# The first x tile of a gated S5/MLP kernel: two feature slabs by plain loads and TensorE transposes, three by one DMA transpose, and W1's first block loaded in two halves

## The chip, the cores and the metric

The kernel runs on one core of a Trainium2 chip. The metric is the device time in microseconds (us) of one execution; lower is better. The kernel before takes a median of 214.95 us in three runs (214.95 to 215.01). In a profile, times are counted from the start of the core's span, and the span is about 1.3 us shorter than the metric.

## The reference

```python
x = A_x                                               # (1, 2048, 640), bf16
g = sigmoid((x * gate_w).sum(-1, keepdims=True))
a = S5(x)        # complex diagonal state-space scan: x @ B, h = Lam*h + u, h @ C, + x * Dskip
b = gelu(x @ w1 + b1) @ w2 + b2                       # w1 (640, 1728), w2 (1728, 640)
return g * a + (1 - g) * b
```

Only the first product matters here: `x @ w1` for the first 512 rows of x. The contraction runs over the 640 features, which must lie on the partitions. So x has to be transposed: five slabs of 128 features by 512 rows.

## The kernel before

All work is put into a list with priorities and estimated durations. A small scheduler orders each engine's instructions at build time, and semaphore waits are put where needed. The parts that the change touches are these (cuts marked `# ...`).

```python
# xT[q]: x tile q transposed, [128, 5 slabs, 512]; xn: x untransposed; FW = 8 * 128 columns of W1
def xtrans(q, ks, prio, dur):        # DMA transpose of the slabs ks, on SP's queue
    load_T(..., [(xT[q][:, ks[0]:ks[-1]+1, :], x2[q*512:(q+1)*512, ks[0]*128:(ks[-1]+1)*128])], ...)

def w1load(k, eng, prio):            # block k of W1: 128 features, 1024 columns, 256 KB
    load(f"w1_{k}", eng, ..., W1sb[:, k, 0:FW], B_w1[k*128:(k+1)*128, 0:FW], [("w1", k)], ...)

w1load(0, "act", -101)
xtrans(0, [0], 0, 1.27)
xtrans(0, [1, 2], 1, 1.27)
w1load(1, "sp", 2)
w1load(2, "sp", 3)
xtrans(0, [3, 4], 4, 1.27)
w1load(3, "sp", 5)
w1load(4, "sp", 6)
# the last 704 columns of W1, all five blocks, 880 KB, in one load:
load("w1_r", "sp", "l_w1r", W1sb[:, :, FW:F], B_w1[:, FW:F].rearrange("(k p) f -> p k f", p=128), [("w1", "r")], ...)
# ... then, on the same queue, the DMA transposes of BT and further loads

def f_warm():                        # eight matmuls on a zeroed tile wz
    for _ in range(8):
        t = nc.tensor.matmul(PS[6][:, :], wz[:, 0:128], wz[:, :], start=True, stop=True)
# ...
def m1_first():                      # stage 1: 40 matmuls, block k outermost, 8 PSUM banks open
    seq = [(k, jf) for k in range(KD) for jf in range(NW)]
    seq.remove((0, NW - 1)); seq.insert(seq.index((1, NW - 1)), (0, NW - 1))
    for k, jf in seq:
        ...  # PS[jf] += W1sb[:, k, jf].T @ xT[0][:, k, :]     needs slab k and block k
def m1(q, j0=0):                     # stage 2 begins with m1(0, 8): the last 704 columns, needs w1_r
    ...
```

I call the matmuls of stage 1 with slab k "k=0" to "k=4", and `w1_r` "W1's last part". PSUM is the memory in which TensorE sums its products, in eight banks. Stage 1 opens all eight at once, so that it can use each slab and block of W1 as it comes. Because k=0 uses seven banks first (bank 7 holds the transposed parameter rows for a while), nine matmuls come between the start of k=1 and that of k=2.

## Time and profile before

| | before |
|---|---|
| median of the runs | 214.95 us |
| TensorE's matmul rows busy | 210.0 of 213.8 us |
| first W1 matmul (k=0) | 4.82 us |
| k=1 starts | 7.39 us |
| k=2 starts | 9.33 us |
| stage 2 starts | 14.51 us |
| W1's last part lands | 13.01 us |

The page of the profile, its line of busy times (PE is TensorE's matmuls, PEld its weight loads, DVE is VectorE, ACT is ScalarE, POOL is GpSimd; further on, SPq is the sync engine issuing DMAs, and "issue" is time for which the profile shows no wait):

```profile
span 213.8 us, 3098 instructions
PE 210.0 (98%) x1257; PEld 119.3 (56%) x1257; DVE 188.3 (88%) x260; ACT 112.9 (53%) x205; POOL 2.5 (1%) x10
```

The chain of waits of the kernel before, restricted to the first 20 us (start in us, length in us, what):

```profile
0.68 0.07 issue
0.75 1.23 SPq L332
1.97 0.06 issue
2.03 1.29 SPq L332
3.32 0.05 issue
3.37 3.89 DMA W1sb<-in_B_w_dram
7.26 0.14 issue
7.39 7.28 PE ps L598 x33
14.67 5.40 PE ps L618 x25
```

L332 is the DMA transpose on SP's queue, L598 is stage 1, and L618 is stage 2. Read it from the top: two transposes are issued, then W1's second block is issued and lands 3.89 us later, and from 7.39 us there is only TensorE, down to 211.61 us.

The waits of TensorE, and its instructions in order of time at the head, say the same (columns of the first: who waits for whom, us in total, times, longest; of the second: start, length, what, and in brackets the idle time before it):

```profile
PE ps L400 <- DVE wz L393: 1.2, 1, 1.2
PE ps L598 <- DMA W1sb<-in_B_w_dram: 0.4, 1, 0.4
```

```profile
4.82 2.13 PE L598 MATMUL ps<-xT,W1sb 128*128 128x512 bf16 x7
6.79 0.22 PE L410 MATMUL ps<-ident,rows 128*128 128x128 bf16 x1
7.39 7.28 PE L598 MATMUL ps<-xT,W1sb 128*128 128x512 bf16 x33 [0.39 <-DMA W1sb<-in_B_w_dram]
14.51 0.81 PE L618 MATMUL ps<-xT,W1sb 128*128 128x512 bf16 x3
```

From 7.39 us on TensorE does not pause: 33 matmuls at 216 ns from start to start end stage 1 at 14.51 us.

Two things are not on a page and are read from the single records of the trace throughout: when each load's last completion event came (its "landing"), and the matmuls' start-to-start times. The latter tell the clock: 427 ns for 512 columns is half rate, 216 ns is full rate. In this profile the last half-rate W1 matmul starts at 5.21 us.

### The profile page before, as it was taken

What the parts mean: (1) busy time and instruction counts of PE and PEld (TensorE: products, weight loads), DVE (VectorE), ACT (ScalarE), POOL (GpSimd) and SP (SyncE); (2) the same over time, 40 slices, a digit from 0 to 9 for tenths busy, and PEclk for the clock granted to TensorE, in tenths of its full rate; (3) what the DMA queues carried; (4) which work ended last, traced back from release to release, by engine and by line L of the source; (5) the groups of instructions that cost most, each with busy time, mean ns of one, the idle gap of its engine ahead of it and who ended that gap; (6) DMA issues with size and microseconds to landing.
All of it is one profiled execution on the core that took longest, in us unless ns stands there. A gap on an engine that the chain in (4) does not pass through costs nothing.

```text
span 213.8 us, 3098 instructions
## 1 busy us (share of the span) xinstructions
PE 210.0 (98%) x1257; PEld 119.3 (56%) x1257; DVE 188.3 (88%) x260; ACT 112.9 (53%) x205; POOL 2.5 (1%) x10
## 2 busy tenths in 40 slices
PE   7999999999999999999999999999999999999995
PEld 2344444444567675444467767444446777677673
DVE  1599999999999899999999999499999999988612
ACT  2569556679525334557835332556786554535230
POOL 1000000000000100000000010000000000000000
PEclk9999999999999999999999999999999999999999
DMA  7999699999000140000000023000000010000011
GB/s 138 297 271 192 142 364 271 224 191 204 0 0 3 61 153 3 31 0 0 0 3 31 0 49 138 32 0 0 3 0 2 0 34 31 31 34 31 31 34 31
DMA packets 30874, 16.35 MB, mean 76 GB/s; under 512 B 23948, under 2 KB 29964, under 8 KB 30860
## 3 DMA queue, kind: packets, MB, share of 16 engines
q1 hardware_dynamic: 30368, 14.57, 28.7%
q0 software_dynamic: 288, 1.31, 2.0%
q10 hardware_dynamic: 204, 0.27, 0.5%
q8 instruction: 10, 0.16, 0.4%
q14 instruction: 4, 0.03, 0.0%
HBM read 7.63 MB, written 2.62 MB: 48 GB/s over the span
## 4 chain that ended last, share of the span: by engine, by line
PE 95%; DMA 2%; SPq 1%; DVE 0%; issue 0%
PE ps L745 26%; PE ps L618 22%; PE ps L791 21%; PE ps L658 20%; PE ps L598 3%; DMA W1sb<-in_B_w_dram 2%; PE ps L759 1%; SPq L332 1%; PE ps L636 1%; DVE osb L824 0%
## 5 line engine op out<-in xcount | busy, mean ns | idle before, releaser
L745 PE MATMUL ps<-W2sb,Gl 128*128 128x320 bf16 x416 | 59.1, 299 | 0.0
L745 PEld LDWEIGHTS ps<-W2sb,Gl 128*128 128x128 bf16 x416 | 40.6, 98 | 16.5 <-ACT Gl L625 0.4
L618 PE MATMUL ps<-xT,W1sb 128*128 128x512 bf16 x220 | 48.1, 379 | 0.0
L791 PE MATMUL ps<-CT,H 128*128 128x320 bf16 x320 | 46.1, 299 | 0.0
L698 DVE TENSOR_TENSOR_SCAN W<-atab,V 128x1280 bf16<-128x1280 f32 x16 | 44.3, 2811 | 0.3
L658 PE MATMUL ps<-xT,BT 128*128 128x512 bf16 x200 | 43.8, 379 | 0.0
L773 ACT ACTIVATE E<-ps,g1col 128x320 bf16<-128x320 f32 x32 | 16.1, 526 | 42.2 <-PE ps L759 18.3
L791 PEld LDWEIGHTS ps<-CT,H 128*128 128x128 bf16 x320 | 30.7, 98 | 13.5 <-issue 1.8
L618 PEld LDWEIGHTS ps<-xT,W1sb 128*128 128x128 bf16 x220 | 21.5, 98 | 25.9
L625 ACT ACTIVATE Gl<-ps,cols 128x512 bf16<-128x512 f32 x44 | 29.7, 691 | 11.5 <-PE ps L618 11.5
L658 PEld LDWEIGHTS ps<-xT,BT 128*128 128x128 bf16 x200 | 19.4, 98 | 23.5 <-ACT Gl L625 0.4
L667 ACT ACTIVATE U<-ps 128x512 bf16<-128x512 f32 x40 | 23.6, 595 | 15.7 <-PE ps L658 15.6
L802 ACT ACTIVATE E<-ps,gcol 128x320 bf16<-128x320 f32 x30 | 15.7, 528 | 16.7 <-PE ps L791 16.6
L732 ACT ACTIVATE ps<-b2b 128x320 f32<-128x320 bf16 x32 | 14.0, 440 | 0.9
L460 DVE TENSOR_TENSOR osb<-xg,E 128x640 bf16<-128x640 bf16 x15 | 7.3, 487 | 7.8 <-ACT E L802 6.8
L810 DVE SCALAR_TENSOR_TENSOR xg<-xn,gcol,dsk 128x640 bf16<-128x640 bf16 x16 | 13.8, 882 | 0.4
L575 DVE SCALAR_TENSOR_TENSOR scr<-xn,gwb 128x640 bf16<-128x640 bf16 x16 | 13.2, 823 | 0.4
L460 DVE TENSOR_TENSOR H<-H,V 128x1280 bf16<-128x1280 bf16 x16 | 12.5, 821 | 0.3
L460 DVE TENSOR_TENSOR V<-V,W 128x1280 bf16<-128x1280 bf16 x16 | 12.5, 821 | 0.3
L460 DVE TENSOR_TENSOR V<-mr,U 128x2560 bf16<-128x2560 bf16 x8 | 11.9, 1489 | 0.2
L460 DVE TENSOR_TENSOR H<-c,W 128x2560 bf16<-128x2560 bf16 x8 | 11.9, 1488 | 0.1
L460 DVE TENSOR_TENSOR V<-s,W 128x2560 bf16<-128x2560 bf16 x8 | 11.9, 1484 | 0.0
(77 smaller groups left out, 101.2 us busy)
## 6 DMA issues: line engine op xcount, KB each, us to landing
out_dram<-osb SPq DMA_DIRECT2D x15, 160.0 KB, 1.8
W2sb<-in_B_w_dram SPq DMA_DIRECT2D x1, 2080.0 KB, 12.2
xn<-in_A_x_dram SPq DMA_DIRECT2D x2, 640.0 KB, 6.4
xn<-in_A_x_dram POOLq DMA_DIRECT2D x2, 640.0 KB, 4.8
W1sb<-in_B_w_dram SPq DMA_DIRECT2D x4, 256.0 KB, 4.1
W1sb<-in_B_w_dram SPq DMA_DIRECT2D x1, 880.0 KB, 6.1
W1sb<-in_B_w_dram ACTq DMA_DIRECT2D x1, 256.0 KB, 2.8
gwb<-in_gate_w_dram SPq DMA_DIRECT2D x1, 160.0 KB, 5.2
```

What stands on the lines that cost most here:

```text
L460: return inc("dve", nc.vector.tensor_tensor(out=o, in0=a, in1=b, op=o_))
L618: t = nc.tensor.matmul(PS[bank][:, :], W1sb[:, k, jf * 128:(jf + 1) * 128], xT[q][:, k, :], start=(k == 0), stop=(k == KD - 1))
L625: return inc("act", nc.scalar.activation(Gl[q % 2][:, jf, :], PS[bank][:, :], ACT.Gelu_apprx_tanh, bias=b1col[:, jf:jf + 1]))
L658: t = nc.tensor.matmul(PS[bank][:, :], BT[:, ci, kd, k * 128:(k + 1) * 128], xT[q][:, kd, :], start=(kd == 0), stop=(kd == KD - 1))
L667: return inc("act", nc.scalar.activation(dst, src, ACT.Copy, scale=1.0 if ci == 0 else -1.0))
L698: t = inc("dve", nc.vector.tensor_tensor_scan(out=g[:, ci, :], data0=a, data1=v[:, ci, :], initial=0.0, op0=ALU.mult, op1=ALU.add))
L732: return inc("act", nc.scalar.activation(PS[bank][:, 0:HALF], b2b[:, cols], ACT.Copy))
L745: t = nc.tensor.matmul(PS[bank][:, 0:HALF], Gl[q % 2][:, jf, t4 * 128:(t4 + 1) * 128], W2sb[:, jf, cols], start=False, stop=False, skip_gr ...
L773: return inc("act", nc.scalar.activation(E1[c % NE][:, cols], PS[bank][:, 0:HALF], ACT.Copy, scale=g1col[:, c:c + 1]))
L791: t = nc.tensor.matmul(PS[bank][:, 0:HALF], H[b % NHB][:, ci, k, s * 128:(s + 1) * 128], CT[:, ci, k, cols], start=(i == 0), stop=(i == 2 ...
L802: return inc("act", nc.scalar.activation(E2[c % NE][:, cols], PS[bank][:, 0:HALF], ACT.Copy, scale=gcol[:, c:c + 1]))
L810: return inc("dve", nc.vector.scalar_tensor_tensor(out=xg[c % 2][:, :], in0=xn[q % 2][:, c % 4, :], scalar=gcol[:, c:c + 1], in1=dsk[:, :] ...
```

## The change

The intent is to start the useful TensorE work earlier. A DMA transpose takes long from issue to landing (4.03 us for slab 0), and the transposes stand in front of W1 in SP's queue. So slabs 0 and 1 are loaded plainly and transposed by TensorE, which is idle then. The other three slabs come by one DMA transpose after W1's blocks 1 and 2. The warm-up matmuls take a constant in place of a zeroed tile and so need not wait.

```diff
-        w1load(0, "act", -101)
-        xtrans(0, [0], 0, 1.27)
-        xtrans(0, [1, 2], 1, 1.27)
-        w1load(1, "sp", 2)
-        w1load(2, "sp", 3)
-        xtrans(0, [3, 4], 4, 1.27)
-        w1load(3, "sp", 5)
-        w1load(4, "sp", 6)
+        KN = 2
+        def xnat(k, prio):           # one slab, untransposed: 512 runs of 256 B
+            load(f"xna{k}", "sp", ..., xn[0][:, :, k*128:(k+1)*128], x2[0:512, k*128:(k+1)*128]...)
+        xnat(0, 0)
+        for h in range(2):           # W1's first block in two halves of 512 columns
+            load(f"w1_0{h}", "sp", ...)
+        xnat(1, 1.2)
+        w1load(1, "sp", 1.3)
+        w1load(2, "sp", 2)
+        xtrans(0, range(KN, KD), 3, 1.8)
+        w1load(3, "sp", 4)
+        w1load(4, "sp", 5)
 ...
-            for _ in range(8): matmul(PS[6], wz, wz)
+            for n in (512, 512, 512, 512, 512, 256): matmul(PS[5][:, 0:n], one, one)
+        for k in range(KN):          # 4 transposes of 128 columns into a PSUM bank, then a copy
+            ... nc.tensor.transpose(pt[:, c*128:(c+1)*128], xn[0][:, c, k*128:(k+1)*128], ident)
+            ... nc.vector.tensor_copy(out=xT[0][:, k, :], in_=pt)
+        ... one filler matmul on the constant, between slab 0's transposes and k=0
 ...
-        xnload(0, "sp", prio=32.4)
+        load("xnb", ...)             # the other three slabs of the untransposed x
```

Behind these loads the queue is unchanged: W1's last part, then the transposes of BT.

More of the change, by code (lines that the diff above doesn't have):

```diff
@@ L350, in w1load @@
             load(f"w1_{k}", eng, f"l_w1{k}", W1sb[:, k, 0:FW], B_w1[k * 128:(k + 1) * 128, 0:FW], [("w1", k)], prio=prio, lat=2.6)
-        w1load(0, "act", -101)
-        xtrans(0, [0], 0, 1.27)
-        xtrans(0, [1, 2], 1, 1.27)
-        w1load(1, "sp", 2)
-        w1load(2, "sp", 3)
-        xtrans(0, [3, 4], 4, 1.27)
-        w1load(3, "sp", 5)
-        w1load(4, "sp", 6)
+        KN = 2
+        def xnat(k, prio):
+            load(f"xna{k}", "sp", f"l_xna{k}", xn[0][:, :, k * 128:(k + 1) * 128],
+                 x2[0:512, k * 128:(k + 1) * 128].rearrange("(c p) d -> p c d", p=128), [("xna", k)], prio, dur=0.45, lat=2.0)
+        xnat(0, 0)
+        for h in range(2):
+            fs = slice(h * FW // 2, (h + 1) * FW // 2)
+            load(f"w1_0{h}", "sp", f"l_w10{h}", W1sb[:, 0, fs], B_w1[0:128, fs], [("w1", 0, h)], 0.1 + h, dur=0.45, lat=2.0)
+        xnat(1, 1.2)
[4 more added lines that the diff above has]
+        w1load(4, "sp", 5)
         load("w1_r", "sp", "l_w1r", W1sb[:, :, FW:F], B_w1[:, FW:F].rearrange("(k p) f -> p k f", p=128), [("w1", "r")], prio=20, lat=5.0)
@@ L388, in bass_gated_mix__ssm_conv_s5__dense_activation_gelu__prompt_kernel, with f_xt, f_xc, f_fill @@
         op("const", "dve", 0.8, ["iota"], ["ident"], f_const, prio=-65)
-        wz = SB("wz", [128, 512], BF16)
-        def f_wz():
-            return inc("dve", nc.vector.memset(wz[:, :], 0.0))
-        op("wz", "dve", 0.35, (), ["wz"], f_wz, prio=-70)
+        one = nc.const_aps.tensor(1.0, [128, 1], BF16)
         def f_warm():
             t = None
-            for _ in range(8):
-                t = nc.tensor.matmul(PS[6][:, :], wz[:, 0:128], wz[:, :], start=True, stop=True)
+            for n in (512, 512, 512, 512, 512, 256):
+                t = nc.tensor.matmul(PS[5][:, 0:n], one.broadcast_to([128, 128]), one.broadcast_to([128, n]), start=True, stop=True)
             return inc("pe", t)
-        op("warm", "pe", 3.2, ["wz"], [("bank", 6)], f_warm, prio=-1000)
+        op("warm", "pe", 2.5, (), [("bank", 5)], f_warm, prio=-1000)
+        for k in range(KN):
+            bank = 7 - k
+            pt = PS[bank][:, :].bitcast(BF16)[:, 0:512]
+            def f_xt(k=k, pt=pt):
+                t = None
+                for c in range(4):
+                    t = nc.tensor.transpose(pt[:, c * 128:(c + 1) * 128], xn[0][:, c, k * 128:(k + 1) * 128], ident[:, :])
+                return inc("pe", t)
+            op(f"xt{k}", "pe", 0.44, [("xna", k), "ident"], [("bank", bank)], f_xt, prio=(-990, 4.5)[k])
+            def f_xc(k=k, pt=pt):
+                return inc("dve", nc.vector.tensor_copy(out=xT[0][:, k, :], in_=pt))
+            op(f"xc{k}", "dve", 0.42, [("bank", bank)], [("xT", 0, k)], f_xc, prio=-2000 + k)
+        def f_fill():
+            return inc("pe", nc.tensor.matmul(PS[5][:, :], one.broadcast_to([128, 128]), one.broadcast_to([128, 512]), start=True, stop=True))
+        op("fill", "pe", 0.4, (), [("bank", 5)], f_fill, prio=-980)
         XT = {q: [("xT", q, k) for k in range(KD)] for q in range(NQ)}
@@ L410, in f_cols @@
             return inc("pe", nc.tensor.transpose(psC, rows[:, :], ident[:, :]))
-        op("cols", "pe", 0.3, list(ROWS) + ["b1b", "ident"], [("bank", 7)], f_cols, prio=7.5)
+        op("cols", "pe", 0.3, list(ROWS) + ["b1b", "ident"], [("bank", 7)], f_cols, prio=9.5)
         def f_cols1():
@@ L547, in bass_gated_mix__ssm_conv_s5__dense_activation_gelu__prompt_kernel @@
         load("gwb", "sp", "l_gwb", gwb[:, :], gate_w.partition_broadcast(128), ["gwb"], prio=32.2)
-        xnload(0, "sp", prio=32.4)
+        load("xnb", "sp", "l_xnb", xn[0][:, :, KN * 128:D], x2[0:512, KN * 128:D].rearrange("(c p) d -> p c d", p=128),
+             [("xn", 0, 0), ("xn", 0, 1)], 32.4, dur=1.0, lat=6.0, reads=[("xna", 0), ("xna", 1)])
         load("w2a", "sp", "l_w2a", W2sb[:, 0:NF - 1, :], B_w2[0:nmain, :].rearrange("(j p) d -> p j d", p=128), ["w2a"], prio=33, lat=8.0)
@@ L599, in f_mm @@
                                                       start=(k == 0), stop=(k == KD - 1)))
-                op(f"m1_0_{jf}_{k}", "pe", d_mm(512), [("xT", 0, k), ("w1", k)], [("bank", jf)] ,
+                op(f"m1_0_{jf}_{k}", "pe", d_mm(512), [("xT", 0, k), ("w1", k) if k else ("w1", 0, jf // (NW // 2))], [("bank", jf)] ,
                    f_mm, prio=pe_prio())
@@ L620, in f_mm @@
                     return inc("pe", t)
-                op(f"m1_{q}_{jf}", "pe", KD * d_mm(512), XT[q] + ([("w1", k) for k in range(KD)] if jf < NW else [("w1", "r")]), [("bank", bank)], f_mm, prio=pe_prio())
+                op(f"m1_{q}_{jf}", "pe", KD * d_mm(512), XT[q] + ([("w1", 0, 0), ("w1", 0, 1)] + [("w1", k) for k in range(1, KD)] if jf < NW else [("w1", "r")]), [("bank", bank)], f_mm, prio=pe_prio())
                 def f_ge(jf=jf, bank=bank):
```

## The prediction

> **What bounds the kernel now.** In the chain of waits TensorE runs from 7.39 us to 211.61 us as an unbroken row of matmul groups (PE is 95% of the chain; the engine table says PE 210.0 of 213.8 us). The view of who waited for whom has only two waits of PE, both in the head. So only the head can move the time: before 7.39 us the chain is two DMA-transpose issues (0.75 to 3.3 us) and the load of W1's second block (issued 3.37, landed 7.26). Later engines have room: each H tile is ready at least 3.2 us before its first matmul, each bias-primed bank at least 3.4 us (times in the trace). What the head saves should arrive whole.
>
> **The head before.** Warm-up matmuls 1.20 to 4.8 us, 427 ns start to start (full clock from 5.76 us). x slab 0 (issued 0.75) lands at 4.78; seven k=0 matmuls 4.81 to 6.8; a wait; k=1 from 7.39. At 216 ns per matmul, nine matmuls later, k=2 starts at 9.33; x slabs 3 and 4 (landed 9.03) are just in time. 24 matmuls of the first stage follow without a gap. The question: when does k=2 start after the change?
>
> **What the change does.** It adds 8 transposes of 128 columns, two PSUM copies on VectorE (estimate 0.4 to 0.6 us each) and one filler matmul, all ahead of the stream that binds. It removes the zeroing of the warm-up tile (warm-up starts about 0.45 us sooner) and two DMA-transpose issues of 1.23 us each at the front of the SP queue. W1's first block moves from ACT's queue to SP in halves.
>
> Estimates from the trace's durations: plain issues cost 0.4 to 0.57 us; the first plain load landed 2.84 us after issue. So:
> - slab 0 (issued 0.75) lands at 3.2 to 3.6; transposed and copied near 4.4.
> - W1's halves land near 3.8 and 4.3, slab 1 near 4.8, W1 block 1 near 5.6 (before 7.26), block 2 near 6.3.
> - k=0 runs 4.4 to 6.6 (partly at half clock), k=1 until about 8.5: TensorE could start k=2 then.
> - The three-slab transpose is issued near 4.05. Before, two slabs landed 4.47 us after issue; a third adds about 0.6 us (512 packets of 256 B, 18 ns each, 16 engines), less some queueing behind W1: landing 8.5 to 9.2. **This, not W1 or slab 0, decides k=2**: about 8.9, against 9.33.
>
> W1 blocks 3 and 4 follow 0.7 us apart and stay ahead of k=3 and k=4, 1.73 us apart.
>
> The Trainium skill ("DMA: Bandwidth & Descriptors", Specifications) asks 512 B or more for line rate; the plain slabs use 256 B runs, so they may be slower than I assume; no run here shows it yet.
>
> **Predicted time.** Saving about 0.45 us: **214.5 us**, range **213.95 to 215.05**. Faster by over 2% 0.01, within 2% 0.98, slower 0.01.
>
> **What would show it.** First W1 matmul near 4.4 us (was 4.81); k=1 near 6.6 (was 7.39) with no wait for W1; a wait for the three-slab transpose before k=2, which starts near 8.9; then one unbroken chain of unchanged length (202.3 us). W1's second block gone from the chain, the transpose in its place.
>
> **What would make it wrong.** Slow 256 B loads, so slab 0 comes no earlier; the three-slab transpose landing after 9.3 (a loss) or before 8.4 (then TensorE's own work decides, saving up to 0.9 us); full clock not granted before 5.8 us, so that k=0 and k=1 run at half rate; VectorE's reordered stages running out of their 3 us of room.

## The result, and the profile after

| | runs | median us | range | ratio to before | 95% interval |
|---|---|---|---|---|---|
| before | 4 | 214.98 | 214.95 to 215.29 | | |
| changed | 4 | 215.07 | 214.76 to 215.18 | 0.9999 | 0.9981 to 1.0016 |

A ratio here is the mean time of one kernel's fast runs (all but those over 1.5% above its fastest) over the mean of the other's fast runs in the same rounds, so it is not quite the ratio of the two medians. The saving of 0.45 us did not show, and the median fell 0.02 us above the top of the predicted range (the ratio, put on the 214.95 us of before, gives 214.93, inside it). The forecast ratio, 214.5 to 214.95 or 0.9979, lies just below the interval.

The profile after is of the execution of 215.18 us. The page's line of busy times has hardly moved:

```profile
span 213.9 us, 3103 instructions
PE 209.4 (98%) x1254; PEld 119.4 (56%) x1264; DVE 188.6 (88%) x261; ACT 113.4 (53%) x205; POOL 2.5 (1%) x10
```

TensorE in order of time at the head; L624 is stage 1 now, L644 stage 2, L415 the slab transposes, L435 the parameter rows:

```profile
4.32 1.04 PE L624 MATMUL ps<-xT,W1sb 128*128 128x512 bf16 x4 [0.15 <-DVE xT L421]
5.19 0.39 PE L415 MATMUL ps<-ident,xn 128*128 128x128 bf16 x4
5.41 1.07 PE L624 MATMUL ps<-xT,W1sb 128*128 128x512 bf16 x3
6.72 0.60 PE L624 MATMUL ps<-xT,W1sb 128*128 128x512 bf16 x2 [0.24 <-DMA W1sb<-in_B_w_dram]
7.17 0.22 PE L435 MATMUL ps<-ident,rows 128*128 128x128 bf16 x1
7.22 7.03 PE L624 MATMUL ps<-xT,W1sb 128*128 128x512 bf16 x30
14.54 0.82 PE L644 MATMUL ps<-xT,W1sb 128*128 128x512 bf16 x3 [0.28 <-DMA W1sb<-in_B_w_dram]
```

The waits of TensorE (two lines left out, 0.8 us before the warm-up and 0.2 us of "issue" later), and the end of the chain's head (same columns as before):

```profile
PE ps L644 <- DMA W1sb<-in_B_w_dram: 0.3, 1, 0.3
PE ps L624 <- DMA W1sb<-in_B_w_dram: 0.2, 1, 0.2
PE ps L624 <- DVE xT L421: 0.2, 1, 0.2
```

```profile
7.30 0.04 issue
7.35 7.14 DMA W1sb<-in_B_w_dram
14.49 0.05 issue
14.54 5.57 PE ps L644 x25
```

The times of the first part came out as forecast. The first W1 matmul starts at 4.32 us (forecast 4.4), k=1 at 6.72 us (6.6), the three-slab transpose lands at 8.85 us, and k=2 starts at 8.89 us (8.9; before 9.33). That is 0.44 us gained. The group of 30 at 7.22 us hides a short pause before k=2; the view merges it.

One of these agreements is luck. The prediction had W1's second block landing near 5.6 us and no wait for W1 at k=1. The block landed at 6.68 us, and TensorE waited for it, as the bracket at 6.72 us shows. That k=1 still came near the forecast is because k=0 was through sooner: no matmul of it ran at half rate, and its seventh started at 6.10 us, so k=1 could have followed at 6.32.

Then comes what the forecast did not have. Stage 1's last matmul starts at 13.87 us, and stage 2 could follow at 14.09 (one step of 216 ns). It starts at 14.53, because the load issued at 7.35 us, W1's last part, took 7.14 us and landed at 14.49. Before, the same load landed at 13.01. The bracket says 0.28 us and not 0.44, because the profile's modelled end of a matmul lies after the next one could start. The gain of 0.44 us at k=2 is given back at stage 2: 14.53 against 14.51 us. From there to the end, both take the same time: 215.15 − 14.51 = 200.64 us before, 215.18 − 14.53 = 200.65 us after.

So the arithmetic fits in one execution of each. The open questions were whether the late landing belongs to the change or to chance, whether removing that wait returns the gain, and whether anything else stands in the way. I had three candidates:

- **Order.** The new order of loads makes W1's last part land late each time.
- **Scatter.** That landing scatters in every kernel; the kernel before has about 1.5 us of room for it in the one profile and the changed one has less.
- **Elsewhere.** The gain is also lost to something other than that landing.

### The profile page after: what moved, and what is told of

It reads as the page before. It is cut to its first block, busy times and chain, and to the rows that moved or that the text cites. A ratio compares the mean times of both kernels' runs of the same rounds, so it can differ in the third digit from the quotient of the medians.

```text
span 213.9 us, 3103 instructions
## 1 busy us (share of the span) xinstructions
PE 209.4 (98%) x1254; PEld 119.4 (56%) x1264; DVE 188.6 (88%) x261; ACT 113.4 (53%) x205; POOL 2.5 (1%) x10
## 4 chain that ended last, share of the span: by engine, by line
PE 92%; DMA 3%; SPq 3%; issue 1%; DVE 0%
PE ps L771 26%; PE ps L644 22%; PE ps L817 21%; PE ps L684 20%; DMA W1sb<-in_B_w_dram 3%; SPq L325 2%; PE ps L785 1%; PE ps L662 1%; SPq L332 1%; DVE osb L850 0%
## 5 line engine op out<-in xcount | busy, mean ns | idle before, releaser
L644 PE MATMUL ps<-xT,W1sb 128*128 128x512 bf16 x215 | 47.6, 379 | 0.5 <-DMA W1sb<-in_B_w_dram 0.3
L684 PE MATMUL ps<-xT,BT 128*128 128x512 bf16 x196 | 43.1, 379 | 0.3 <-issue 0.2
L644 PEld LDWEIGHTS ps<-xT,W1sb 128*128 128x128 bf16 x220 | 21.5, 98 | 26.5 <-DMA W1sb<-in_B_w_dram 0.8
L651 ACT ACTIVATE Gl<-ps,cols 128x512 bf16<-128x512 f32 x44 | 29.8, 690 | 11.9 <-PE ps L644 11.9
L485 DVE TENSOR_TENSOR V<-mr,U 128x2560 bf16<-128x2560 bf16 x8 | 11.9, 1490 | 0.2
L485 DVE TENSOR_TENSOR H<-c,W 128x2560 bf16<-128x2560 bf16 x8 | 11.9, 1488 | 0.1
L485 DVE TENSOR_TENSOR V<-s,W 128x2560 bf16<-128x2560 bf16 x8 | 11.9, 1484 | 0.0
```

The costliest lines, as they stand in the source:

```text
L485: return inc("dve", nc.vector.tensor_tensor(out=o, in0=a, in1=b, op=o_))
L644: t = nc.tensor.matmul(PS[bank][:, :], W1sb[:, k, jf * 128:(jf + 1) * 128], xT[q][:, k, :], start=(k == 0), stop=(k == KD - 1))
L651: return inc("act", nc.scalar.activation(Gl[q % 2][:, jf, :], PS[bank][:, :], ACT.Gelu_apprx_tanh, bias=b1col[:, jf:jf + 1]))
L684: t = nc.tensor.matmul(PS[bank][:, :], BT[:, ci, kd, k * 128:(k + 1) * 128], xT[q][:, kd, :], start=(kd == 0), stop=(kd == KD - 1))
```

## The experiments

All kernels gave correct results. The three calls ran on two chips: runs 1 to 8 on one, 9 to 12 on another.

### 1 and 2. b_again and a_again: both kernels unchanged, second profiles

> The kernel before, unchanged, for a second profile. Both theories: 214.95 to 215.0 us. Theory A (the last part of W1 lands late only because of the changed order of loads): it lands near 13.0 us again, 1.5 us ahead of the matmuls that need it at 14.5. Theory B (the landing of that part scatters from execution to execution whatever the order): it lands somewhere from 12.9 to 14.5, and the total does not move, because there is 1.5 us of room.

> The changed kernel, unchanged, for a second profile. k=2 starts at 8.9 us again, the first W1 stage ends at 14.08, and the total is about 200.5 us plus the later of 14.08 and the landing of W1's last part. Theory A: that landing is again at 14.3 to 14.5 and the total 215.0. Theory B: the landing differs by several tenths of a us from 14.49, and the total of that execution follows it, down to 214.5 where it lands before 14.08.

| | median us | range | ratio | interval | profiled execution | k=2 | last part lands | stage 2 |
|---|---|---|---|---|---|---|---|---|
| b_again | 215.11 | 215.02 to 215.21 | 0.9991 | 0.9976 to 1.0006 | 215.17 | 9.27 | 13.54 | 14.45 |
| a_again | 214.75 | 214.62 to 214.92 | 0.9977 | 0.9960 to 0.9994 | 214.62 | 8.80 | 13.79 | 13.99 |

(b_again's stage 2 start is worked out as the last record of stage 1, 14.23 us, plus one step of 216 ns, as one matmul's record is missing.) The landing moved by 0.5 us in the kernel before and by 0.7 us in the changed one, so it does scatter. In a_again it came before TensorE needed it, and the execution took 214.62 us, near the 214.5 forecast. The view of TensorE's waits in a_again lists no load at all. (It leaves out pauses under 150 ns, such as the one of 0.14 us before k=2, after the transpose's landing at 8.76 us.)

```profile
PE ps L403 <- PEq L959: 0.8, 1, 0.8
PE ps L684 <- issue: 0.2, 1, 0.2
```

In this set the changed kernel was faster by 0.23%; in the first set it was not, and run 5, on this same chip, did not repeat it.

### 3. a_split: W1's last part in two loads

The experiment takes the exposure away, and not the wait alone: the first 256 of the 704 columns come by themselves, so the next 10 matmuls need only those.

```diff
-        load("w1_r", ..., W1sb[:, :, FW:F], ..., [("w1", "r")], prio=20)
+        FR = FW + 256
+        load("w1_ra", ..., W1sb[:, :, FW:FR], ..., [("w1", "ra")], prio=20)
+        load("w1_r", ..., W1sb[:, :, FR:F], ..., [("w1", "r")], prio=20.1)
 # groups 8 and 9 of stage 2 depend on "ra", the others on "r"
```

> The changed kernel, with W1's last part (704 columns) loaded by two loads, 256 columns for the next two groups of matmuls first, then the rest. If the wait for W1's last part is what ate the gain: the 256 columns land before 13.5 us, no wait of TensorE at 14.1, the chain is unbroken from 8.9 us, 214.5 us (0.45 below before). If the gain was lost elsewhere (VectorE's order, banks, the end): 215.0 us again.

Measured: fast runs of 214.42, 214.92 and 215.14 us, ratio 0.9978 (0.9956 to 1.0000). The profiled execution took 316.36 us at a granted clock of 0.659; it is a slow one and I use no time of it.

### 4. a_split_act: the halves of W1's first block from ACT's queue

```diff
-            load(f"w1_0{h}", "sp", ..., 0.1 + h, ...)
+            load(f"w1_0{h}", "act", ..., -102 + h / 2, ...)
```

> As a_split, and W1's first block in its two halves from ACT's queue again, so that everything behind it on SP's queue is issued about 1 us earlier. If the three-slab transpose's issue time sets k=2: it is issued near 2.9 us instead of 3.9 and lands near 8.0; W1's second block lands near 6.0 instead of 6.7; k=2 then starts when TensorE is done with k=1, near 8.2 to 8.4, and the total is 213.9 to 214.1 us. If the transpose is bound by the data moved before it and not by its issue, it lands at 8.7 to 8.9 again and the total stays at 214.5.

Measured: 216.08 us (215.94 to 216.22), ratio 1.0036 (1.0021 to 1.0051), which is slower, clear of the noise, and a miss of both expectations. The waits of TensorE:

```profile
PE ps L437 <- DMA rows<-in_B_b_dram: 1.3, 1, 1.3
PE ps L417 <- DMA xn<-in_A_x_dram: 0.7, 1, 0.7
```

The three-slab transpose was issued at 2.81 us, 1.1 us sooner than in the changed kernel, but landed at 8.57, only 0.28 us sooner. The Trainium skill says, in "DMA: Bandwidth & Descriptors", section "Issuing engines are not separate DMA queues", that loads issued from several engines run on the same 16 DMA engines, so that a second queue saves only issue time. This trace agrees: 1.1 us of issue saved, 0.28 us of landing. What the move cost is a side effect. The small parameter loads stand behind W1's halves on ACT's queue; the last landed at 8.40 us in place of 5.71. The transpose of those rows stands in the middle of k=1 in TensorE's order, so the whole of stage 1 waited for it, and k=2 started at 10.10 us. Slab 0 also landed at 3.90 us in place of 3.14. So in this profile the bulk loads ahead of the transpose, and not its issue, set most of its landing, and in this kernel a load of a few hundred bytes can hold the head.

### 5. a_five: the changed kernel a third time

> The changed kernel, unchanged, timed beside the others. So far it gave a median of 215.07 us on one chip and 214.75 on another, against 214.98 and 215.21 for the kernel before. If its gain exists and is eaten in part of the executions by the landing of W1's last part: 214.55 where that part lands before 14.08 us in the profile, up to 215.2 where it lands later; median 214.6 to 215.0, 0.1 to 0.4 us below the kernel before. If there is no gain at all: the same as the kernel before within 0.1 us, and k=2 no earlier than 9.3 us.

Measured: 214.92 us median of 7 (214.61 to 216.55), before 215.03 of 11 (214.31 to 215.47), ratio 0.9998 (0.9978 to 1.0019). The profile fell on the 216.55 us execution, which is the clearest case of all. The waits of TensorE, then its instructions around the wait:

```profile
PE ps L644 <- DMA W1sb<-in_B_w_dram: 1.6, 1, 1.6
PE ps L624 <- DMA xT<-in_A_x_dram: 0.2, 1, 0.2
```

```profile
13.00 1.24 PE L624 MATMUL ps<-xT,W1sb 128*128 128x512 bf16 x5
15.82 1.04 PE L644 MATMUL ps<-xT,W1sb 128*128 128x512 bf16 x4 [1.58 <-DMA W1sb<-in_B_w_dram]
```

k=2 started at 8.88 us, as before, but W1's last part landed at 15.77 us. Stage 2 started at 15.81 and the execution ended 200.74 us later.

### 6. a_split5: the split again

The edit is that of a_split.

> a_split again, because its profile fell in a slow execution. If the late landing of W1's last part is the only thing between the changed kernel and its gain: the chain unbroken from k=2 (8.8 to 8.9 us) on, and the times bunched at 214.4 to 214.6 us. If other loads scatter as much (the second block of W1, the three-slab transpose): k=2 itself scatters from 8.7 to 9.3 us, and the times lie between 214.4 and 215.1 us, no better than a_five by more than 0.2 us.

Measured: 214.58 us (214.29 to 215.00), ratio 0.9984 (0.9965 to 1.0003). The first 256 columns landed at 12.73 us and the rest at 14.37. The rest was as late as in the first profile after, but now nothing waited for it: stage 2 started at 13.98 us and the profiled execution took 214.62 us. TensorE's waits (without the warm-up's and one of "issue", as before), and its instructions where stage 1 (L626) meets stage 2 (L646), now without a wait:

```profile
PE ps L626 <- DVE xT L423: 0.2, 1, 0.2
PE ps L626 <- DMA W1sb<-in_B_w_dram: 0.2, 1, 0.2
```

```profile
12.69 1.46 PE L626 MATMUL ps<-xT,W1sb 128*128 128x512 bf16 x6
13.99 1.46 PE L646 MATMUL ps<-xT,W1sb 128*128 128x512 bf16 x6
```

Both waits lie before k=2. An unsplit load landing at 14.37 us would have cost this execution 0.4 us (an estimate, 14.37 less 13.98). So with the wait at stage 2 gone, the forecast time comes out in this profile. The median lies 0.34 us below a_five, but the intervals overlap, and the runs spread over 0.7 us, not bunched as the first expectation had it.

### 7. b_split: the same split in the kernel before

The same diff as in 3, applied to the kernel before.

> The kernel before with the same split of W1's last part, as a control. The kernel before has 0.9 to 1.5 us of room there (landing 13.0 and 13.5 us, needed at 14.5), so the split should do nothing: ratio 1.000 within 0.1%, k=1 again begins when W1's second block lands, at 7.2 to 7.4 us. If the split helps by itself (say, through how the loads share the engines), the ratio falls by 0.1% or more here too.

Measured: 215.05 us (214.80 to 215.50), ratio 1.0008 (0.9988 to 1.0027). Nothing, as expected where there is room. The split is not a gain by itself. k=1 started at 7.18 us, with W1's second block landing at 7.04.

### 8. kn3: three slabs by plain loads

```diff
-        KN = 2
+        KN = 3
         w1load(1, "sp", 1.3)
+        xnat(2, 1.4)
         w1load(2, "sp", 2)
 # slab 2's transposes share bank 7 and come in k=1; the parameter rows' transpose moves behind them
```

> a_split with a third x slab by a plain load and TensorE transposes, so that the DMA transpose brings two slabs, needed one block of W1 later. If the three-slab transpose (landing 8.6 to 8.9 us) is what holds k=2 in the changed kernel: k=2 starts at 8.5 us or a little before, when TensorE is through with k=1 and 0.22 us of transposes, and the time is 0.2 to 0.5 us below a_split5. If W1's blocks hold k=2: no wait for x, a wait for W1's third block in its place, and no gain.

Measured: 214.85 us (214.63 to 215.10), ratio 0.9996 (0.9978 to 1.0014). It was not below a_split5, which had 214.58. k=2 did start earlier, at 8.63 us, with no wait for x. The next gate stood behind it: the chain at the head of kn3 shows a pause before k=3,

```profile
7.91 2.62 PE ps L627 x12
10.52 0.04 issue
10.56 1.24 PE ps L627 x5
```

and W1's fourth block landed at 10.42 us, 0.1 us before. Stage 2 started at 14.00 us, as in a_split5 (13.98). The loads as a whole pace the head; moving one gate uncovers the next.

### 9. a_third: the changed kernel, on the other chip

> The changed kernel once more, for the scatter. k=2 at 8.8 to 8.9 us; the time of the profiled execution is its landing of W1's last part or 14.0, whichever is later, plus 200.5 us; the runs lie between 214.5 and 215.5 us, with a median near 214.9.

Measured: 215.20 us (214.51 to 215.54), before 214.95 of 11 (214.55 to 215.24), ratio 1.0008 (0.9992 to 1.0024). The profiled execution (215.17 us) broke the expectation, and this brought in the third candidate. W1's last part landed early, at 13.45 us, and the three-slab transpose at 8.62 us, the earliest of the four profiles of this kernel. TensorE waited for no load. Yet stage 2 started at 14.54 us. TensorE in order of time:

```profile
4.30 1.89 PE L624 MATMUL ps<-xT,W1sb 128*128 128x512 bf16 x4
5.98 0.63 PE L415 MATMUL ps<-ident,xn 128*128 128x128 bf16 x4
6.41 1.55 PE L624 MATMUL ps<-xT,W1sb 128*128 128x512 bf16 x5
7.79 0.22 PE L435 MATMUL ps<-ident,rows 128*128 128x128 bf16 x1
7.85 6.85 PE L624 MATMUL ps<-xT,W1sb 128*128 128x512 bf16 x31
14.54 0.81 PE L644 MATMUL ps<-xT,W1sb 128*128 128x512 bf16 x3
```

Compare the first line with the profile after: four matmuls in 1.89 us here, in 1.04 us there. Here they start 427 ns apart, at half rate, and the last half-rate matmul starts at 6.41 us. k=0 took so long that TensorE itself reached k=2 only at 9.36 us. The clock was granted late, which the prediction had named as a risk.

The Trainium skill, "TensorE: Matmul & The Clock Gate", Part 1, says that the full clock comes after about 3.4 us of activity, seen through a free-running window, so that the moment varies from run to run. The traces agree on the variation, less on the length. The four profiles of this one kernel have 0, 2, 0 and 5 half-rate matmuls in stage 1. Their matmuls began at 0.78 us, and the clock records in the traces have the full clock from 5.13 us in a_again, 4.46 in a_five and 6.84 in a_third (the profile after has no such record): 3.7 to 6.1 us after the first matmul, with short pauses between. The kernel before had 2 and 1, and there a wait of 0.4 to 0.8 us for W1's second block follows and absorbs them.

### 10. a_split_b: the split once more, beside a_third

The edit is that of a_split.

> a_split once more, on the same chip as a_third. If the split takes the scatter of W1's last part off the chain: median 214.5 to 214.7 us, 0.2 to 0.4 below a_third, and no run above 215.1. If the 214.58 of before was luck: the same as a_third.

Measured: 214.92 us (214.77 to 215.14), ratio 1.0000 (0.9988 to 1.0012). The median lies 0.28 us below a_third, but above the expected 214.5 to 214.7, and it equals the kernel before on this chip. In its profile W1's last part was not waited for; W1's second block landed at 6.89 us and the three-slab transpose at 9.04, so k=2 started at 9.09. The rest of that part landed at 13.30 us, a microsecond before stage 2, so this execution may not have needed the split. The split removes one of several scattering gates.

### 11. a_split_t: the three-slab transpose undone into one and two slabs

```diff
-        xtrans(0, range(KN, KD), 3, 1.8)
+        xtrans(0, [2], 3, 1.27)
+        xtrans(0, [3, 4], 3.1, 1.27)
```

> a_split with the three-slab transpose undone into slab 2 alone and slabs 3 and 4 together. If the landing of the three-slab transpose is what k=2 waits for: slab 2 lands near 8.0 to 8.3 us, k=2 starts when TensorE is through with k=1, near 8.55 to 8.6 (0.2 to 0.3 us sooner), slabs 3 and 4 land near 9.0, before k=3 needs them at 10.3, and the time falls by 0.2 us. If the transposes are held up as a whole by the data ahead of them: slab 2 no earlier than 8.6, and no gain.

Measured: 214.88 us (214.62 to 215.00), ratio 0.9993 (0.9981 to 1.0005). Slab 2 landed at 7.81 us, sooner than expected, and the other two at 8.76. But this execution had four half-rate W1 matmuls, so TensorE reached k=2 only at 9.06 us, with no wait for a load:

```profile
4.23 1.87 PE L627 MATMUL ps<-xT,W1sb 128*128 128x512 bf16 x4
6.16 1.50 PE L627 MATMUL ps<-xT,W1sb 128*128 128x512 bf16 x5
7.55 2.32 PE L627 MATMUL ps<-xT,W1sb 128*128 128x512 bf16 x10
```

So the transpose's landing does fall by taking one slab alone, but the gain in time is inside the noise.

### 12. a_split_wz: the old warm-up tile

```diff
-   matmul(PS[5][:, 0:n], one.broadcast_to([128, 128]), one.broadcast_to([128, n]))
+   matmul(PS[5][:, 0:n], wz[:, 0:128], wz[:, 0:n])      # waits for VectorE to zero wz, as before
```

> a_split with the warm-up on a zeroed tile, as before the change, so that TensorE's first instructions start about 0.45 us later. If only the loads that end the head matter: the first W1 matmul moves from 4.3 to about 4.7 us and k=2 stays at 8.8 to 8.9, the time equal to a_split_b within 0.1 us. If an earlier start of TensorE or of its full clock is part of the gain: 0.2 to 0.4 us slower than a_split_b.

Measured: 215.05 us (214.54 to 215.54), ratio 1.0007 (0.9992 to 1.0022), so 0.13 us above a_split_b, between the two expectations: inconclusive by time. In its profile (215.54 us) the first W1 matmul started at 4.66 us and five W1 matmuls ran at half rate, the last started at 6.77 us. TensorE's only wait is that for the warm-up tile:

```profile
PE ps L411 <- DVE wz L404: 1.2, 1, 1.2
```

k=2 started at 9.72 us, after the transpose had landed at 9.34, so TensorE's own pace held it. Whether a warm-up started earlier brings the full clock earlier on average can't be told from one profile.

## Why the prediction was right or wrong

These are all the profiles of the two kernels. The last column shows that everything is decided before stage 2.

| profile | half-rate matmuls in stage 1 | k=2 starts | last part lands | stage 2 starts | time | time less stage 2 |
|---|---|---|---|---|---|---|
| before | 2 | 9.33 | 13.01 | 14.51 | 215.15 | 200.64 |
| b_again | 1 | 9.27 | 13.54 | 14.45 | 215.17 | 200.72 |
| changed | 0 | 8.89 | 14.49 | 14.53 | 215.18 | 200.65 |
| a_again | 2 | 8.80 | 13.79 | 13.99 | 214.62 | 200.63 |
| a_five | 0 | 8.88 | 15.77 | 15.81 | 216.55 | 200.74 |
| a_third | 5 | 9.36 | 13.45 | 14.54 | 215.17 | 200.63 |

- **Right: nothing behind the head matters.** The time from stage 2's start to the end is 200.63 to 200.74 us in all six. VectorE's reordered stages cost nothing.
- **Right: k=2 is the point to watch, near 8.9 us, and the three-slab transpose decides it.** In three of the four profiles of the changed kernel k=2 starts within 0.05 us of that transpose's landing (8.85, 8.76, 8.84 us). It gained 0.4 to 0.5 us.
- **Right, and worth little: 256-byte runs are slower, but it does not matter here.** The skill ("DMA: Bandwidth & Descriptors", Specifications) asks for 512 B and more, and the trace agrees: 256 B took 18 ns on an engine and 2 KB took 84 ns, so 14 against 24 bytes per ns. Slab 0 still landed 2.40 us after its issue, where the DMA transpose took 4.03. In b_split and a_split5 the packets of 512 B took 27 ns, 19 bytes per ns, so at 512 B the rate of 2 KB is not reached yet. (All these are medians over packets.)
- **Wrong: "What the head saves should arrive whole", and from k=2 on "one unbroken chain of unchanged length (202.3 us)".** The 24 matmuls of stage 1 from k=2 on did follow without a gap; the chain broke behind them, at stage 2. The prediction checks the room of the H tiles, the banks and W1's blocks 3 and 4, but does not mention W1's last part, which stage 2 needs and which had landed 1.5 us early in the one profile. In the profile after it landed at 14.49 us, when TensorE was ready at 14.09: 0.44 us, the whole gain. In a_five it cost 1.7 us. Split, it cost nothing (a_split5), and the same split in the kernel before did nothing (b_split).
- **Wrong: "W1 block 1 near 5.6" and "k=1 near 6.6 (was 7.39) with no wait for W1".** W1's second block landed at 6.68 us in the profile after (6.43 to 6.48 in the other three), and the third at 7.33 where 6.3 was forecast. k=1 came at 6.72 us all the same, because the full clock came early in that execution: two errors that cancelled. (In a_again, with two half-rate matmuls, k=1 came at 6.66 us and did not wait, as forecast.)
- **A named risk that came true: the late full clock.** In a_third the half-rate matmuls alone put k=2 back at 9.36 us.
- **The size.** k=2 gained about the forecast 0.45 us in three profiles of four, but the total has three gates: TensorE's own pace until the full clock, the transpose, and W1's last part. The latest of the three counts, and all scatter: the transpose landed at 8.62 to 8.85 us in these four profiles, the last part at 13.45 to 15.77, and the half-rate matmuls number 0 to 5. A forecast that takes one profile's landing for each gate is the best case, and it came out in one profile of four. Over all runs the changed kernel's mean is 215.05 us (21 runs) and the kernel before's 215.01 (33 runs), pooled over the four sets and so only roughly comparable.

**Order or scatter?** W1's last part landed at 13.01 and 13.54 us in the kernel before, and at 14.49, 13.79, 15.77 and 13.45 in the changed one. Scatter is shown, and less room is shown. That the new order also makes it later on average is not shown by two values against four. (Split, with the later of the two loads counted: 13.17 us in b_split, 14.37 and 13.30 in a_split5 and a_split_b.) The trace's packets say what a late landing looks like: of the 640 packets of this load, nine tenths had ended by 11.92 us before and by 12.48 after, but the last at 12.65 and 14.04. So a few of the 16 DMA engines seem to lag, and the load is as late as its slowest engine. The skill's "DMA: Bandwidth & Descriptors", section "Why a DMA increments its semaphore by 16 and not by 1", says that only the full count means that all data has landed, and this agrees: the first of the 16 completions came at 12.66 us, the last at 14.49. The packets also show where the time goes. The load was issued 0.1 to 0.8 us later in the changed kernel (7.04 to 7.68 us against 6.92 and 6.96), but its first packet started at 9.4 to 9.8 us in all six profiles. What differs is that some packets were held up: of 640, which mostly took 60 ns, 0 and 6 took over 100 ns in the kernel before, and 24, 9, 28 and 22 in the changed one (in the order of the table), the longest 0.94 us. This leans towards **Order**, but the split kernels do not bear it out each time: 5 of 1280 packets in b_split, 18 in a_split5, 1 in a_split_b. What holds these packets up stays open; the records do not name the engine of a packet.

**A better version?** The changed kernel with the split has the lowest mean, 214.77 us over 14 fast runs in three sets, about 0.24 us below the kernel before, but each of its intervals reaches 1.0. kn3 and a_split_t are no better. I would keep the split, since it removes a wait that the traces show, and would not claim a gain for it.

## What to carry to other kernels

Room in a profile is one draw: before counting on an earlier start, list every later load that the earlier work will meet, with the time between its landing and its first use, and set against it how far such landings scatter between executions. A large load whose first columns are needed soon can be split at the point of need: here this took the wait away (12.73 us for the first columns, 14.37 for the rest, in a_split5), though the medians show no gain that is clear of the noise. A forecast that comes out should be checked step by step: here k=1 was on time for the wrong reason. When several gates lie within half a microsecond of each other, removing one moves the time by less than its wait, because the latest of the others takes over.

## What the Trainium skill lacked or had wrong

- "TensorE: Matmul & The Clock Gate", Part 1, gives the moment of the full clock as varying by ±500 ns from run to run; its counts of cold matmuls in the same section (6, 11 or 14) allow more. Here, in four profiles of one unchanged kernel whose matmuls began at 0.78 us each time, stage 1 had 0, 2, 0 and 5 half-rate matmuls. The clock records have the full clock from 5.13, 4.46 and 6.84 us in three of them, a spread of 2.4 us. Whether the short transposes and pauses of these kernels have a part in that was not tested; there is one of about 0.3 us between the filler and k=0 (in the profile after, the filler starts at 3.59 us and k=0 at 4.32; a matmul at half rate takes 0.43).
- "DMA: Bandwidth & Descriptors" has no figure for how unevenly the 16 engines finish one load. Here one 880 KB load took 6.1 to 8.1 us from issue to landing in six executions, with nine tenths of its packets done by 11.9 to 13.3 us and the last by 12.7 to 15.3.
- The same page tells that an engine's completion waits for that engine's earlier writes. It does not say what the trace of the profile after shows: 15 of the load's 4-byte packets, which I take for its completions, were sent from 11.86 to 13.22 us, but all but two of the completion counts arrived at 14.28 us or later, just after the 256-byte packets of the DMA transpose queued next, stalled from 12.3 us, had ended at 14.24 to 14.28. The other five profiles show the same: the stalled packets end at 12.84 to 15.54 us, and all of the load's completion counts, or all but one, come within 0.3 us after. So a following DMA transpose seems to hold back an earlier load's completions; but the stalled packets themselves end about 0.2 us after the load's last data packet, so both may wait for the slowest engine. It explains little of the late landing: from the load's last data packet to its landing it is 0.36 to 0.47 us, and 0.32 to 0.35 us for W1's fifth block, which has a plain load behind it. None of this was tested by itself.
- No page has the time from issue to landing of a small DMA transpose against a plain load of the same bytes. Here, for 128 KB first in the queue: 4.03 us (3.73 in a second execution) against 2.40 us (2.31).
